# A constant two-part inverse stage on array quarters, with its twiddle factors moved into the last stage's table

## The chip, the cores and the metric

One core of one Trainium2 chip. The metric is the device time of one execution in microseconds (us). The kernel runs on one core, so there is no second die to compare; the granted TensorE clock stands beside each profile.

## The reference

The input is 8 batches of 3008 positions with 256 features. Each batch is mixed along the positions by a filter in the frequency domain, and a two-layer network with a hard swish follows. All data are float32.

```python
def _attn_ref(x, filt_r, filt_i):            # x (8, 3008, 256)
    X = np.fft.rfft(x, axis=1)
    F = (filt_r + 1j * filt_i)[None, :, :]
    y = np.fft.irfft(X * F, n=x.shape[1], axis=1)
    return y.astype(np.float32)

def _moe_ref(x, w_in, w_out):                # x (24064, 256), w_in (256, 2048)
    h = x @ w_in
    g = h * np.clip(h + 3.0, 0.0, 6.0) / 6.0
    return (g @ w_out).astype(np.float32)
```

## The kernel before

The transforms are factored, 3008 = 47 x 64. Going forward, a 47-point stage (`a_unit`, the "first stage") is followed by a 64-point stage (`b_unit`, the "second stage"). VectorE multiplies by the filter (`f_unit`, `y_unit`). Going back, `bi_unit` is the 64-point stage and `n_unit` the 47-point stage (the "last stage"), which writes straight into the network's input `xn`. Between the two inverse stages the data go through memory: `g_store` writes `g_tmp`, `t4_load` reads it back in another order.

Batch 0 is transformed ahead of everything ("the start"). Then the network runs as a loop of 376 steps (47 blocks of 512 tokens, 8 steps each), and the transforms of batches 1 to 7 are placed unit by unit into its steps. What the argument touches:

```python
psF = pool("psF", 2, space=PSUM)   # two banks, shared by a, b, bi and n units in the loop
wai = const.tile([P, TOK], FP32, name="wai")          # last stage, one table for all columns
...
def table_load(b, c):               # 4 frequencies: filter, wb and wi, three buffers each
    ...
    wi = tabp.tile([P, TC, P], FP32, name="wi")
    nc.sync.dma_start(wi, wi_d[:, ts(c, TC), :])
    st["tab", b, c] = wb, wi
...
def a_unit(b, c):                   # first stage: four 64x64 quarters of the array, two banks
    xc = x_tile(b, c)
    t = t1p.tile([P, 2, XC // 2, D], FP32, name="t1")
    ps = [bank(b) for h in range(2)]
    for g in range(2):
        for h in range(2):
            nc.tensor.matmul(ps[h][ts(g, 64)], wa[ts(h, 64), ts(g, 64)],
                             xc[ts(h, 64), 2 * g:2 * g + 2, :], start=True, stop=True)
    for h in range(2):
        nc.scalar.activation(out=t[:, h, :, :], in_=ps[h], func=AXT.Copy)
...
def bi_unit(b, i):                  # inverse second stage: 2 frequencies, own table each
    y = st.pop(("y", b, i))
    c, r = divmod(2 * i, TC)
    ps = psF.tile([P, 2, D], FP32, name="psf", tag="f")
    for u in range(2):
        nc.tensor.matmul(ps[:, u, :], st["tab", b, c][1][:, r + u, :], y[:, u, :], start=True, stop=True)
    if r == 0:
        st["t3", b, c] = t3p.tile([P, TC, D], FP32, name="t3")
    nc.scalar.activation(out=st["t3", b, c][:, r:r + 2, :], in_=ps, func=AXT.Copy)
...
# the loop's schedule of one batch (k: block in which its tokens are first used)
b_at = [(k - 2 - j // 3) * NP + 6 - 2 * (j % 3) for j in u]
bi_at = [i + 3 for i in b_at]
a_at = [(k - 7 + c // 4) * NP + (0, 2, 5, 7)[c % 4] for c in range(NB)]
if n == 1:                          # batch 1 has less room and is packed densely
    a_at = list(range(NB))
    b_at = [10 + 7 * i // 4 for i in range(NU)]
    bi_at = [i + 3 for i in b_at]
```

## Time and profile before

| | before |
|---|---|
| three runs, median (range) | 2824.01 us (2823.33 to 2826.01) |
| profiled run | 2821.93 us, span 2820.1 us, granted clock 0.982 |
| start, up to the first matmul of the loop | 133.76 us |
| loop steps 0 to 8; 8 to 34 (batch 1); 34 to 375 (batches 2 to 7) | 77.12; 195.38; 2383.19 us |
| rest | 30.68 us |

The stretches are differences between the starts of loop steps, and a step starts with the first matmul that reads `xn` into `al`. These five terms add up to the span.

From the table of groups with each shape kept apart: line, engine, operation, output<-inputs, tile, count, then busy us and mean ns of one, then the idle time ahead of them and its releasers. The first is the unit that is changed, the second the first-stage unit of the same shape as the new one, the third the eviction.

```profile
L305 PE MATMUL psf<-y,wi 128*128 128x256 f32 x384 | 106.0, 401 | 25.7 <-DVE y L297 17.9 <-issue 7.9
L252 PE MATMUL psf<-xs,wa 64*64 64x512 f32 x448 | 68.7, 623 | 0.0
L308 ACT ACTIVATE t<-psf 128x512 f32<-128x512 f32 x96 | 57.3, 597 | 102.7 <-PE psf L305 99.7 <-DMA g_tmp<-t 3.0
```

The idle 25.7 us before L305 is mostly in the start, where TensorE waits for VectorE. Busy time of quarter matmuls overlaps (448 records in 68.7 us, though one takes 623 ns), so what such a unit costs must be read from the step it sits in.

### The profile page before, as it was taken

Reading aid. Unit: us, or ns where it says so; the run is one execution under the profiler, and the core shown is the slowest. Engines: PE = TensorE matmul, PEld = TensorE weight load, DVE = VectorE, ACT = ScalarE, POOL = GpSimd, SP = SyncE. Lnnn points to the kernel's source line nnn. Section 1 sums busy time; section 2 is a strip of 40 time slices with the busy share of each in tenths; the row PEclk is TensorE's granted clock in tenths of the full one; section 3 lists DMA queues with packets and bytes.
Section 4 is the critical chain, followed back from the end, with each engine's and each line's share of the span. In section 5 each row is a group of like instructions: output and inputs, shape, how many; then the busy total and the mean of one; then the engine's idle time right before and its main releaser. Section 6 shows DMA issues by size and latency. Waiting matters only on the chain.

```text
span 2820.1 us, 47236 instructions
## 1 busy us (share of the span) xinstructions
PE 2713.0 (96%) x18096; PEld 2461.9 (87%) x18096; DVE 1991.3 (71%) x3463; ACT 1329.8 (47%) x2672; POOL 437.3 (16%) x621
## 2 busy tenths in 40 slices
PE   4589999999999999999999999999999999999997
PEld 1369898999889998899988999899998999999996
DVE  6787865777657776677756777567775677766665
ACT  1144455444554445544455444544455444444443
POOL 6470012000120011201021101210012100000000
PEclk7699999999999999999999999999999999999998
DMA  8543223311223222422134211342113421100000
GB/s 241 160 121 104 79 58 104 103 54 54 81 73 101 59 65 70 105 68 80 40 86 108 68 60 45 88 112 75 48 48 92 110 67 47 42 24 24 17 8 16
DMA packets 127817, 211.89 MB, mean 75 GB/s; under 512 B 22280, under 2 KB 86600, under 8 KB 127592
## 3 DMA queue, kind: packets, MB, share of 16 engines
q1 hardware_dynamic: 103892, 150.54, 18.9%
q0 software_dynamic: 19104, 52.46, 6.5%
q10 hardware_dynamic: 4596, 5.88, 0.6%
q8 instruction: 143, 2.34, 0.3%
q14 instruction: 82, 0.67, 0.1%
HBM read 133.81 MB, written 74.97 MB: 74 GB/s over the span
## 4 chain that ended last, share of the span: by engine, by line
PE 92%; DMA 3%; DVE 2%; POOL 1%; issue 1%; ACT 0%; SPq 0%; ACTq 0%; POOLq 0%; DVEq 0%
PE po L440 41%; PE al L364 23%; PE be L364 17%; PE psn L339 4%; PE psf L305 3%; PE psf L277 3%; PE psf L252 2%; DMA z_tmp<-t 1%; DMA xn<-in_x_dram 1%; DMA ft<-in_filt_i_dram 0%; DMA xs<-in_x_dram 0%; DVE y L296 0%; ACT t L255 0%; DVE y L297 0%; DVE s L291 0%
## 5 line engine op out<-in xcount | busy, mean ns | idle before, releaser
L440 PEld LDWEIGHTS po<-w_out,g 128*128 128x128 f32 x10528 | 1402.0, 192 | 123.0 <-DVE g L422 31.6
L440 PE MATMUL po<-w_out,g 128*128 128x128 f32 x10528 | 1426.6, 276 | 5.0 <-DVE g L414 4.6
L414 DVE SCALAR_TENSOR_TENSOR g<-r,h 128x512 f32<-128x512 f32 x752 | 518.3, 689 | 255.7 <-ACT r L409 242.8
L409 ACT ACTIVATE r<-h,half_c 128x512 f32<-128x512 f32 x752 | 542.5, 721 | 318.0 <-DVE h L390 305.7
L364 PE MATMUL al<-xt,w_in 128*128 128x256 f32 x2256 | 676.0, 382 | 6.6 <-DVE h L395 4.4
L390 DVE TENSOR_TENSOR h<-be,s 128x512 f32<-128x512 f32 x376 | 259.7, 691 | 277.8 <-PE be L364 271.6
L364 PE MATMUL be<-xn,w_in 128*128 128x256 f32 x1504 | 447.8, 379 | 0.0
L364 PEld LDWEIGHTS al<-xt,w_in 128*128 128x128 f32 x2256 | 342.9, 192 | 10.2 <-DVE h L395 4.5
L404 ACT ACTIVATE h<-al 128x256 f32<-128x256 f32 x376 | 144.0, 383 | 375.9 <-PE al L364 375.9
L364 PEld LDWEIGHTS be<-xn,w_in 128*128 128x128 f32 x1504 | 286.2, 190 | 38.9
L395 DVE TENSOR_TENSOR h<-al,s 128x256 f32<-128x256 f32 x376 | 159.4, 424 | 192.9 <-PE al L364 192.5
L422 DVE TENSOR_TENSOR g<-g 128x512 f32<-128x512 f32 x376 | 260.3, 692 | 12.9
L385 ACT ACTIVATE s<-al 128x256 f32<-128x256 f32 x376 | 144.3, 384 | 202.1 <-PE al L364 202.1
L376 ACT ACTIVATE s<-be 128x256 f32<-128x256 f32 x376 | 144.0, 383 | 182.6 <-PE be L364 182.6
L364 PE MATMUL al<-xn,w_in 128*128 128x256 f32 x752 | 225.2, 381 | 0.5 <-ACT h L404 0.5
L364 PE MATMUL be<-xt,w_in 128*128 128x256 f32 x752 | 224.3, 380 | 0.8 <-POOL xt L357 0.8
L265 POOL DMA_DIRECT2D z_tmp<-t x224 | 132.7, 595 | 426.7 <-ACT t L255 423.7
L424 DVE TENSOR_TENSOR g<-g 128x256 f32<-128x256 f32 x376 | 168.8, 449 | 12.8
L375 ACT ACTIVATE s<-al 128x256 f32<-128x256 f32 x376 | 144.0, 383 | 70.8 <-PE al L364 70.7
L421 DVE TENSOR_TENSOR g<-g 128x256 f32<-128x256 f32 x376 | 161.9, 430 | 12.8
L364 PEld LDWEIGHTS be<-xt,w_in 128*128 128x128 f32 x752 | 143.0, 190 | 20.8 <-POOL xt L357 1.6
L357 POOL TENSOR_TENSOR xt<-xn 128x256 f32<-128x256 f32 x94 | 71.4, 759 | 495.0 <-ACT xn L345 495.0
(71 smaller groups left out, 1825.3 us busy)
## 6 DMA issues: line engine op xcount, KB each, us to landing
t<-z_tmp SPq DMA_DIRECT2D x48, 512.0 KB
t<-g_tmp SPq DMA_DIRECT2D x188, 120.0 KB
z_tmp<-t POOLq DMA_DIRECT2D x224, 96.0 KB, 2.9
g_tmp<-t POOLq DMA_DIRECT2D x42, 512.0 KB, 3.4
out_dram<-o SPq DMA_DIRECT2D x328, 47.0 KB
xs<-in_x_dram SPq DMA_DIRECT2D x120, 128.0 KB
ft<-in_filt_r_dram SPq DMA_DIRECT2D x96, 128.0 KB
ft<-in_filt_i_dram SPq DMA_DIRECT2D x96, 128.0 KB
```

The source lines that it names most:

```text
L364: nc.tensor.matmul(ps, w_in[p][:, w, :], x, start=start, stop=stop, skip_group_check=True)
L375: nc.scalar.activation(out=s[:, 0, :], in_=al, func=AXT.Copy)
L376: nc.scalar.activation(out=s5, in_=be[:, 1, :], func=AXT.Copy)
L385: nc.scalar.activation(out=s[:, 1, :], in_=al, func=AXT.Copy)
L390: nc.vector.tensor_tensor(out=st["h"][0].rearrange("p (a n) -> p a n", a=2), in0=be, in1=s, op=ALU.add)
L395: nc.vector.tensor_tensor(out=st["h"][1][:, 256:512], in0=al, in1=s5, op=ALU.add)
L409: nc.scalar.activation(out=r, in_=st["h"][i], func=AXT.Relu, bias=half_c, scale=1.0 / 6.0)
L414: nc.vector.scalar_tensor_tensor(out=st["g", k, p][:, o:o + 2, :].rearrange("p a n -> p (a n)"), in0=st["r", i], scalar=1.0, in1=st["h"][i ...
L421: v.tensor_tensor(out=g[:, G1, :], in0=g[:, G3, :], in1=g[:, G22, :], op=ALU.add)
L422: v.tensor_tensor(out=g[:, G3:G2 + 1:2, :], in0=g[:, G3:G1 + 1, :], in1=g[:, G11:G11 + 1, :].broadcast_to([P, 2, 256]), op=ALU.subtract)
L424: v.tensor_tensor(out=g[:, G4, :], in0=g[:, G12, :], in1=g[:, G2, :], op=ALU.subtract)
L440: nc.tensor.matmul(st["po", k][bank][:, part, u, :], g[:, a, ts(u, P)], w_out[p][:, w, :], start=(p == 0 and n in OPENS and u == 0), stop= ...
```

## The change

The old inverse 64-point stage multiplied the two parts (real and imaginary) of each frequency by a 128x128 table of its own, because the twiddle factors were folded in. The change leaves them out of this stage. What stays is one constant table, `wi` [128, 64], of 33 cosine and 31 sine columns: its upper 64 rows multiply the real half of `y`, its lower 64 rows the imaginary half, and the two results are kept apart. So one pair of units (four frequencies) becomes four 64x64 matmuls over 512 columns, one on each quarter of the array. The two row halves write two PSUM banks, and the pair therefore takes both banks of the pool. (The Trainium skill, "TensorEngine Tiling (Array Packing)", section Gotcha 1: PSUM Pressure, says that row tiles must write different banks.) The twiddles, and the sums and differences that put columns c and 64 - c back together, go into the last stage's table `wai`, which now has 32 slices, one for each such pair of columns.

```diff
-    wai = np.zeros((P, TOK))
+    wai = np.zeros((P, HC, TOK))          # HC = 32 columns, twiddles inside
-    wi = np.zeros((P, KH, P))
+    wi = np.zeros((P, NC))                # rows of the real half over rows of the imaginary half
...
-    g_d = nc.dram_tensor("g_tmp", (B, KH, P, D), FP32, kind="Internal").ap()
+    g_d = nc.dram_tensor("g_tmp", (B, NU, 2, 2, NC, D), FP32, kind="Internal").ap()
...
     def bi_unit(b, i):
-        y = st.pop(("y", b, i))
-        ...
-        ps = psF.tile([P, 2, D], FP32, name="psf", tag="f")
-        for u in range(2):
-            nc.tensor.matmul(ps[:, u, :], st["tab", b, c][1][:, r + u, :], y[:, u, :], start=True, stop=True)
-        ...
-        nc.scalar.activation(out=st["t3", b, c][:, r:r + 2, :], in_=ps, func=AXT.Copy)
+        ys = [st.pop(("y", b, i + v)) for v in range(2)]
+        ps = [psF.tile([P, 2, D], FP32, name="psf", tag="f") for ri in range(2)]
+        for v in range(2):
+            for ri in range(2):
+                nc.tensor.matmul(ps[ri][ts(v, 64)], wi[ts(ri, 64), :], ys[v][ts(ri, 64)], start=True, stop=True)
+        t = t3p.tile([P, 2, 2, D], FP32, name="t3")
+        for ri in range(2):
+            nc.scalar.activation(out=t[:, ri, :, :], in_=ps[ri], func=AXT.Copy)
+        st["t3", b, i] = t
...
     def g_store(b, i, q=None):
-        q.dma_start(g_d[b, ts(c, TC), :, :].rearrange("k p d -> p k d"), st.pop(("t3", b, c)))
+        for v in range(2):
+            q.dma_start(g_d[b, i + v].rearrange("ri u c d -> c (ri u) d"), t[ts(v, 64)].rearrange("p ri u d -> p (ri u) d"))
...
     def t4_load(i, k0=0, k1=KH):
-                nc.sync.dma_start(t4[i % 2][p0 + k0:p0 + k1, 0:n, :], g_d[b, k0:k1, ds(ri * NC + h * HC + j, n), :])
+                nc.sync.dma_start(t4[i % 2][p0 + k0:p0 + k1, 0:n, :].rearrange("k j d -> k (j d)"),
+                                  g_d[b, k0 // 2:k1 // 2, ri, :, ds(h * HC + j, n), :].rearrange("i u j d -> i u (j d)"))
...
     def n_unit(i, dh):
-            nc.tensor.matmul(ps[:, ts(q, TOK)], t4[i % 2][:, q, ts(dh, P)], wai, start=True, stop=True)
+            nc.tensor.matmul(ps[:, ts(q, TOK)], t4[i % 2][:, q, ts(dh, P)], wai[:, chunks[i][1] + q, :], start=True, stop=True)
```

The rest (cut): filter and `wb` tables have two buffers in place of three and no `wi` load, `wai` is loaded once (1.5 MB), output rows are written through `outer(j, h)`, and in batches 2 to 7 the pair is placed alone in its step.

More of the change, by code (lines that the diff above doesn't have):

```diff
@@ L35 @@
 TB = 3
+FB = 2
+T3B = 2
 NU = KH // 2
@@ L42, with outer @@
 RING = 3 * BLK
+def outer(j, h):
+    return (NC - j if j else HC) if h else j
 def _make_tables():
@@ L55, in _make_tables @@
                 wa[h * 64:h * 64 + NA, g * 64 + 32 + k] = -np.sin(th)
-            m = 2.0 if k else 1.0
-            wai[h * 64 + k, h * NA:(h + 1) * NA] = m * np.cos(th)
-            wai[h * 64 + 32 + k, h * NA:(h + 1) * NA] = -m * np.sin(th)
     wb = np.zeros((P, KH, P))
-    wi = np.zeros((P, KH, P))
+    wi = np.zeros((P, NC))
     re, im = slice(0, NC), slice(NC, P)
@@ L70, in _make_tables @@
             wb[re, k, HALF + q], wb[im, k, HALF + q] = -sn, sign * cs
-            wi[q, k, re], wi[q, k, im] = cs, sign * sn
-            wi[HALF + q, k, re], wi[HALF + q, k, im] = -sn, sign * cs
+    for q in range(64):
+        g, sign = (q, 1.0) if q < 32 else (31 - q, -1.0)
+        co, si = (f([2 * np.pi * ((j * g) % NC) / NC for j in range(HC + 1)]) for f in (np.cos, np.sin))
+        ab = np.concatenate([co, np.zeros(HC - 1) if q == 63 else si[1:HC]])
+        wi[q], wi[HALF + q] = ab, sign * ab
+    for j in range(HC):
+        for h in range(2):
+            to = slice(h * NA, (h + 1) * NA)
+            for k in range(KH):
+                m = 2.0 if k else 1.0
+                th = 2 * np.pi * ((a * k * NC + outer(j, h) * k) % N) / N
+                cs, sn = m * np.cos(th), m * np.sin(th)
+                s = -1.0 if h else 1.0
+                if j:
+                    wai[k, j, to], wai[32 + k, j, to] = cs, -sn
+                    wai[64 + k, j, to], wai[96 + k, j, to] = -s * sn, -s * cs
+                else:
+                    wai[h * 64 + k, j, to], wai[h * 64 + 32 + k, j, to] = cs, -sn
     f = np.float32
@@ L105 @@
     t2p = pool("t2p", TB)
-    tabp = pool("tabp", TB)
+    tabp = pool("tabp", FB)
     sp = pool("sp", 2)
     yp = pool("yp", 3)
-    t3p = pool("t3p", 2)
+    t3p = pool("t3p", T3B)
     xtp = pool("xtp", 2)
@@ L120 @@
     wa = const.tile([P, P], FP32, name="wa")
-    wai = const.tile([P, TOK], FP32, name="wai")
+    wai = const.tile([P, HC, TOK], FP32, name="wai")
+    wi = const.tile([P, NC], FP32, name="wi")
     xs = [const.tile([P, XC, D], FP32, name="xs%d" % i) for i in range(3)]
-    ft = [const.tile([P, TC, D], FP32, name="ft%d" % i) for i in range(TB)]
+    ft = [const.tile([P, TC, D], FP32, name="ft%d" % i) for i in range(FB)]
     t4 = [const.tile([P, NJ, D], FP32, name="t4%d" % i) for i in range(2)]
@@ L137, in table_load @@
     def table_load(b, c):
-        t = ft[(b * NT + c) % TB]
+        t = ft[(b * NT + c) % FB]
         for src, p0 in ((filt_r, 0), (filt_i, HALF)):
@@ L144, in table_load @@
         nc.sync.dma_start(wb, wb_d[:, ts(c, TC), :])
-        wi = tabp.tile([P, TC, P], FP32, name="wi")
-        nc.sync.dma_start(wi, wi_d[:, ts(c, TC), :])
-        st["tab", b, c] = wb, wi
+        st["wb", b, c] = wb
     NCONV = 16
@@ L276, in b_unit @@
         for u in range(2):
-            nc.tensor.matmul(ps[:, u, :], st["tab", b, c][0][:, r + u, :],
+            nc.tensor.matmul(ps[:, u, :], st["wb", b, c][:, r + u, :],
                              st["t2", b, c][:, r + u, :], start=True, stop=True)
@@ L283, in f_unit @@
         ps = st.pop(("ps", b, i))
-        f = ft[(b * NT + c) % TB][:, r:r + 2, :]
+        f = ft[(b * NT + c) % FB][:, r:r + 2, :]
         s1 = sp.tile([P, 2, D], FP32, name="s1")
@@ L300, in bi_unit, with g_store @@
     def bi_unit(b, i):
-        y = st.pop(("y", b, i))
-        c, r = divmod(2 * i, TC)
-        ps = psF.tile([P, 2, D], FP32, name="psf", tag="f")
-        for u in range(2):
-            nc.tensor.matmul(ps[:, u, :], st["tab", b, c][1][:, r + u, :], y[:, u, :], start=True, stop=True)
-        if r == 0:
-            st["t3", b, c] = t3p.tile([P, TC, D], FP32, name="t3")
-        nc.scalar.activation(out=st["t3", b, c][:, r:r + 2, :], in_=ps, func=AXT.Copy)
-    def g_store(b, c, q=None):
+        ys = [st.pop(("y", b, i + v)) for v in range(2)]
[7 more added lines that the diff above has]
+        st["t3", b, i] = t
+    def g_store(b, i, q=None):
         q = q or nc.gpsimd
-        q.dma_start(g_d[b, ts(c, TC), :, :].rearrange("k p d -> p k d"), st.pop(("t3", b, c)))
+        t = st.pop(("t3", b, i))
+        for v in range(2):
+            q.dma_start(g_d[b, i + v].rearrange("ri u c d -> c (ri u) d"), t[ts(v, 64)].rearrange("p ri u d -> p (ri u) d"))
     chunks = []
@@ L479, in out_5 @@
             m = min(NA - a, P - p)
-            nc.sync.dma_start(raw(out, b * N + a * NC + h * HC + j, [[NC * D, m], [1, D]]),
+            nc.sync.dma_start(raw(out, b * N + a * NC + outer(j, h), [[NC * D, m], [1, D]]),
                               o[p:p + m, t % BLK // P, :])
@@ L527 @@
         convert(6)
+        nc.sync.dma_start(wi, wi_d)
         for c in range(TB):
             t2_load(0, c)
-            if c:
+            if 0 < c < FB:
                 table_load(0, c)
-        nc.sync.dma_start(wai, wai_d)
         for t in t4:
@@ L542 @@
             if i:
-                bi_unit(0, i - 1)
                 if i % 2 == 0:
+                    bi_unit(0, i - 2)
                     c = i // 2 - 1
-                    g_store(0, c, nc.scalar)
+                    g_store(0, i - 2, nc.scalar)
+                    if c + FB < NT:
+                        table_load(0, c + FB)
+                    if c == 0:
+                        nc.sync.dma_start(wai, wai_d)
                     if c + TB < NT:
                         t2_load(0, c + TB)
-                        table_load(0, c + TB)
                     if c == NT - 2:
@@ L585, in places @@
             b_at = [(k - 2 - j // 3) * NP + 6 - 2 * (j % 3) for j in u]
-            bi_at = [i + 3 for i in b_at]
+            bi_at = [b_at[i] + (5 if i % 6 == 1 else 3) for i in range(NU)]
             a_at = [(k - 7 + c // 4) * NP + (0, 2, 5, 7)[c % 4] for c in range(NB)]
@@ L602 @@
                 elif n > 1:
-                    at(max(prev[0][c + NB - 3], s - 6), x_load, n, c)
+                    at(max(prev[c + NB - 3], s - 6), x_load, n, c)
             for c in range(NT):
-                s = bi_at[2 * (c - TB) + 1] if c >= TB else a_at[-1] + 1
-                if n > 1 and c < TB:
-                    s = max(s, prev[1][2 * (NT + c - TB) + 1])
+                s = b_at[2 * (c - TB) + 1] + 1 if c >= TB else a_at[-1] + 1
+                at(s, t2_load, n, c)
+                s = b_at[2 * (c - FB) + 1] + 1 if c >= FB else a_at[-1] + 1
                 at(s, table_load, n, c)
-                at(s, t2_load, n, c)
             for i in range(NU):
@@ L613 @@
                 at(b_at[i] + 1, y_unit, n, i)
-                at(bi_at[i], bi_unit, n, i)
                 if i % 2:
-                    at(bi_at[i], g_store, n, i // 2)
-            prev = a_at, bi_at
+                    at(bi_at[i], bi_unit, n, i - 1)
+                    at(bi_at[i], g_store, n, i - 1)
+            prev = a_at
         items = [(k, p) for k in range(NBLK) for p in range(NP)]
```

## The prediction

> **What bounds the kernel now.** I read the granted clock first: one core, 0.982, so no throttled state to correct for. Then the busy totals, the slices and the chain of work that ended last.
>
> ```profile
> PE 2713.0 (96%) x18096; PEld 2461.9 (87%) x18096; DVE 1991.3 (71%) x3463; ACT 1329.8 (47%) x2672; POOL 437.3 (16%) x621
> ...
> PE   4589999999999999999999999999999999999997
> ...
> PEclk7699999999999999999999999999999999999998
> ...
> PE 92%; DMA 3%; DVE 2%; POOL 1%; issue 1%; ACT 0%; SPq 0%; ACTq 0%; POOLq 0%; DVEq 0%
> ```
>
> TensorE is full from the fourth slice (about 210 us) to the last; only the first three slices are set by something else. The table of stretches says it sharper: TensorE is busy 25.44 of 30 us in 180 to 210, 30.00 of 30 in 210 to 240, and 500.00 of 500 in each of the three stretches from 1000 to 2500. So after 210 us a TensorE nanosecond removed is a nanosecond won, unless a new wait takes its place; before 210 us it isn't.
>
> What the concerned step costs I read from the order of time of TensorE. The main loop has 376 steps, each starting with the first matmul of L364 that reads xn into al. Four such starts, with what stands between:
>
> ```profile
> 1002.04 0.60 PE L364 MATMUL al<-xn,w_in 128*128 128x256 f32 x2
> ...
> 1009.05 0.60 PE L364 MATMUL al<-xn,w_in 128*128 128x256 f32 x2
> ...
> 1010.35 1.03 PE L305 MATMUL psf<-y,wi 128*128 128x256 f32 x4
> 1011.22 0.61 PE L440 MATMUL po<-w_out,g 128*128 128x128 f32 x4
> ...
> 1016.07 0.60 PE L364 MATMUL al<-xn,w_in 128*128 128x256 f32 x2
> ...
> 1022.21 0.60 PE L364 MATMUL al<-xn,w_in 128*128 128x256 f32 x2
> ```
>
> A step with one inverse unit (L305, two matmuls, four records) lasts 7.02 us, a step with nothing extra 6.14. Over all steps after the 30th the medians are 6.148 plain (86 steps), 7.012 with an inverse unit (71), 7.265 with a last-stage unit L339 of five columns, 7.365 with a first-stage unit L252 (41). Within a class they agree to some 0.001 us (one plain step is 0.06 longer): the loop has no slack and no noise. So one inverse unit costs 0.864 us, one first-stage unit 1.217.
>
> The first-stage unit matters because the new inverse unit has exactly its shape: four 64x64 by 512 matmuls, one on each quarter of the array, the two row halves into two PSUM banks.
>
> ```profile
> 840.63 0.59 PE L364 MATMUL be<-xn,w_in 128*128 128x256 f32 x2
> 841.15 1.09 PE L252 MATMUL psf<-xs,wa 64*64 64x512 f32 x8
> 842.17 0.71 PE L440 MATMUL po<-w_out,g 128*128 128x128 f32 x4
> 842.72 0.60 PE L364 MATMUL al<-xt,w_in 128*128 128x256 f32 x2
> ```
>
> From be to L252 pass 0.52 us where the usual step is 0.43, and from L440 to al 0.55 where it is 0.44: entering and leaving quarter mode costs some 0.2 us, the eight records 1.02.
>
> **What the skill says.** The Trainium skill, "TensorEngine Tiling (Array Packing)", section Key Properties, says that changing the tiling mode drains the array and that tiles operate independently: the two 0.1 us gaps and the 1.02 us for eight records agree. The same page, section PSUM Bottleneck, says that tiling speeds TensorE but not the emptying of PSUM: the 128x512 ACT evictions stay as many as they are (96 of 0.597 us on L308), and no run yet shows whether they delay. The Trainium skill, "FP8 and Floating Point Precision", section TensorE Precision Notes, gives true FP32 four passes through the array; with 262 cycles for 256 columns at 2.4 GHz ("TensorE: Matmul & The Clock Gate", section Back-to-back issue gap) two passes make 218 ns, and this trace has 0.864/4 = 216 ns per record, two records per matmul. It agrees.
>
> **The change part by part.** *Removed*: 84 inverse units after the first batch (7 batches of 12), each 0.864 us. *Added*: 42 pair units, each four quarter matmuls. Multiplications halve; by passes the four quarters need 2 records x 427 ns = 0.853 us if all run at once, against 1.728 for two old units. I take not that but the measured twin: 1.217 us. A pair saves 1.728 - 1.217 = 0.511 us. *Moved*: the twiddles go into the last stage's moving operand, which gets a different slice per column but the same shape 128x94, so L339 stays at 1.117 us for five. VectorE work is unchanged; evictions are as many and as large. Stores to g become 84 of 64 partitions in place of 42 of 128, the bytes the same, from GpSimd, which is 16% busy. Table loads lose wi (48 loads of 256 KB) and their buffers go from three to two; in the loop a table is asked for seven or more steps (over 40 us) ahead, so that costs nothing. wai grows from 47 KB to 1.5 MB, loaded once in the first stage, where six wi loads of the same total disappear.
>
> *Batches 2 to 7*: the schedule puts all 36 pairs alone in their step. 36 x 0.511 = 18.4 us saved.
>
> *Batch 1* is packed more densely. Counting which units share a step, five of its six pairs meet another user of the two-buffer PSUM pool in the same step (two behind a last-stage unit, two ahead of a second-stage unit, one ahead of a first-stage unit). A pair takes both buffers, so someone waits for an ACT eviction. The trace prices that: last-stage plus first-stage in one step lasts 9.229 where the sum is 6.148 + 1.117 + 1.217 = 8.482, a wait of 0.747. Removed 12 x 0.864 = 10.4, added 6 x 1.217 = 7.3 plus 5 x 0.75 = 3.8: a loss of about 0.7. That stretch also shows VectorE waits (steps 24 to 26), so I book a loss of 0.5.
>
> *Start, before 210 us.* From 60 to 118 us VectorE is nearly gapless (filter products and weight conversion), so TensorE's gain there is nothing. Its end is a serial chain:
>
> ```profile
> 117.86 0.70 DVE y L297
> ...
> 118.69 1.12 PE psf L305 x4
> ...
> 119.83 0.60 ACT t L308
> ...
> 120.46 3.74 DMA g_tmp<-t
> ...
> 124.55 2.77 DMA t<-g_tmp
> ```
>
> The pair now ends with two evictions after the last y instead of one (+0.6), two stores issued 0.4 us apart instead of one, and, from the order of the changed program, ten instead of eight small loads behind that store (2 x 0.34 us). GpSimd's conversion runs beside it and hides some. I book a loss of 1.5 us. The filter tables with two buffers: the third chunk's can be issued when VectorE leaves the first (66 us), is needed at 79.6, and a load takes 5 to 7 us here; no wait.
>
> Sum: 2824.0 - 18.4 + 0.5 + 1.5 = 2807.6 us, 0.6% less.
>
> **The rivals.**
> 1. *The PSUM pool eats the gain everywhere.* Twelve of the 36 pairs follow directly on a step with a second-stage unit, whose buffer VectorE frees only with its third product:
>
> ```profile
> 1051.95 0.69 DVE L291 TENSOR_TENSOR s<-psf,ft 64x512 f32<-64x512 f32 x1
> ...
> 1052.93 1.03 PE L305 MATMUL psf<-y,wi 128*128 128x256 f32 x4
> ```
>
> The buffer is free at 1052.64, 0.29 us before the pair would start; VectorE to TensorE hand-over is about 0.15 (79.60 to 79.75 in the start). It fits, narrowly. Were it missed by 0.3 us each time, 4 us go: 2811. Two evictions in a row on ACT (1.2 us) before the next step's s could also hold L390; against it, first-stage units evict twice too and their steps show the plain sum. If every pair waited the 0.75, the change would lose 36 x 0.24 = 9 us: 2833 or so.
> 2. *The start gets slower.* Two filter buffers, and loads that wait on the completion of a store eight transfers back, as the fourth chunk's load does now (its second quarter waits 6.4 us until 73.5). If the larger wai transfer or the later paired stores delay each of the last three tables by 3 us, 2816. For it: that stretch moves 250 GB/s at 0.86 DMA share. Against: every need I could date has 5 us or more of slack.
> 3. *Better than the twin.* If the quarters came at their pass count plus a mode change (0.85 + 0.2), a pair saves 0.66, and 36 give 24: 2802. The twin's own count speaks against it.
>
> **Range and chances.** The body is a product of two durations that do not scatter, so most of the spread is the start (about 4 us either way) and rival 1. Range 2800 to 2816. For 2% the kernel would have to lose or gain 56 us, three times all that the changed unit can save; even the removal of every inverse matmul would save but 84 x 0.864 = 73. Faster by over 2%: 0.01; within: 0.97; slower: 0.02.
>
> **What would show each step.** A step with a pair alone at 7.36 us (7.0 to 7.3 would favour rival 3, 8.1 rival 1); the new inverse rows at about 42 x 1.2 us beyond the start; pairs directly behind a second-stage unit no longer than the others; waits of first bank writes on ACT evictions only in steps 14, 18, 25, 28 and 32; the main loop's first matmul at 135 us rather than 133.8 (140 or more would be rival 2); the three 500 us stretches holding the same 100% TensorE. The prediction is wrong if the pair's step isn't 7.36, or if the first 210 us move by more than 4.

## More of the kernel before

The loads that read `g_tmp` back, all issued by SyncE, with the issue times of one in ns (min/median/max):

```profile
L333 SPq DMA_DIRECT2D t<-g_tmp x236: 239/362/1230, 117.9 to 2622.2; - x118
```

## The result, and the profile after

| | before | after |
|---|---|---|
| median of 4 runs (range) | 2823.67 us (2823.21 to 2826.01) | 2807.19 us (2805.65 to 2807.47) |
| ratio to before, 95% interval | | 0.9939 [0.9922, 0.9956]: within 2% |
| profiled run, granted clock | 2821.93 us, 0.982 | 2807.47 us, 0.987 |
| start | 133.76 | 138.21 |
| steps 0 to 8 | 77.12 | 75.35 |
| steps 8 to 34 (batch 1) | 195.38 | 196.50 |
| steps 34 to 375 | 2383.19 | 2364.89 |
| rest | 30.68 | 30.74 |

The kernel is 0.6% faster, and the gain has one place: steps 34 to 375, 18.30 us. The start up to step 8 gave back 213.56 - 210.88 = 2.68 us and batch 1 1.12 us.

The page of the changed kernel: TensorE is as full as before, with 13 us less work, and the chain of work that ended last is TensorE by the same 92%.

```profile
PE 2700.1 (96%) x18096; PEld 2395.8 (85%) x18096; DVE 1993.9 (71%) x3463; ACT 1325.9 (47%) x2672; POOL 456.4 (16%) x663
...
PE   3589999999999999999999999999999999999997
...
PEclk9699999999999999999999999999999999999998
...
PE 92%; DVE 3%; DMA 2%; ACT 1%; issue 1%; POOL 0%; SPq 0%; ACTq 0%; POOLq 0%; DVEq 0%
```

The count of TensorE records is the same, 18096, because two records per 256-column matmul became two per 512-column quarter matmul; only their kind changed. Memory reads fell from 133.81 to 122.75 MB, which the table loads account for, and no time follows from that, as the experiments show.

The order of time of TensorE in the changed kernel, around a step that holds a pair and nothing else (start us, duration us, engine, line, operation, output<-inputs, tile, count):

```profile
1013.55 0.60 PE L392 MATMUL al<-xn,w_in 128*128 128x256 f32 x2
...
1019.70 0.60 PE L392 MATMUL al<-xn,w_in 128*128 128x256 f32 x2
...
1020.56 0.59 PE L392 MATMUL be<-xn,w_in 128*128 128x256 f32 x2
1021.09 1.09 PE L329 MATMUL psf<-y,wi 64*64 64x512 f32 x8
1022.11 0.71 PE L468 MATMUL po<-w_out,g 128*128 128x128 f32 x4
1022.66 0.60 PE L392 MATMUL al<-xt,w_in 128*128 128x256 f32 x2
...
1027.06 0.60 PE L392 MATMUL al<-xn,w_in 128*128 128x256 f32 x2
```

The plain step lasts 6.15 us, the step with the pair 7.36. The 0.53 us from `be` to L329 and 0.55 from L468 to `al` are, within 0.01 us, those that the prediction read around the first-stage unit. Over all 36 steps with a pair alone the duration is 7.364 to 7.365 us, also for those right behind a step with a second-stage unit. No step of the loop beyond batch 1 waits for anything new.

The groups of the changed kernel, in the order of those shown of before:

```profile
L329 PE MATMUL psf<-y,wi 64*64 64x512 f32 x384 | 73.0, 648 | 13.9 <-DVE y L319 13.7 <-DVE s L314 0.3
L275 PE MATMUL psf<-xs,wa 64*64 64x512 f32 x448 | 68.4, 623 | 0.7 <-ACT t L332 0.7
L332 ACT ACTIVATE t<-psf 128x512 f32<-128x512 f32 x96 | 52.8, 596 | 95.6 <-PE psf L329 83.8 <-DMA ft<-in_filt_r_dram 11.3
```

The unit's busy time fell from 106.0 to 73.0 us, and its twin L275 stays as it was. The 0.7 us before L275 waiting for L332 is one shared step of batch 1.

What batch 1 pays is seen in its step 25, which starts at 339.55 and lasts 10.32 us, where the sum of its parts is 6.148 + 1.217 + 0.864 = 8.23. The order of time of TensorE in the changed kernel, with the idle time and its releaser in brackets:

```profile
339.55 0.60 PE L392 MATMUL al<-xn,w_in 128*128 128x256 f32 x2
...
340.94 1.07 PE L329 MATMUL psf<-y,wi 64*64 64x512 f32 x2
342.27 1.08 PE L329 MATMUL psf<-y,wi 64*64 64x512 f32 x6 [0.27 <-DVE s L314]
344.05 1.13 PE L300 MATMUL psf<-t,wb 128*128 128x256 f32 x4 [0.69 <-ACT t L332]
```

The pair gets its first bank and then waits for VectorE to free the second, which a second-stage unit still holds. The next second-stage unit (L300) waits 0.69 us for the pair's eviction. The five steps with such a meeting, 14, 18, 25, 28 and 32, exceed the sum of their parts by 0.75, 1.09, 2.09, 0.69 and 1.05 us. Of this, 0.67 us in step 25 and 0.75 in step 32 were there before the change. Steps 17, 19 and 26 exceed theirs by 0.60, 0.69 and 1.66 us in both kernels.

In the start, the chain of work that ended last, in order of time, from the last pair on (start us, us, what):

```profile
119.20 2.70 PE psf L329 x4
...
121.93 0.60 ACT t L332
...
122.55 3.29 DMA g_tmp<-t
...
125.86 0.73 SPq L360
...
126.64 0.73 SPq L360
...
127.41 0.65 SPq L360
...
128.11 0.61 SPq L360
...
128.77 0.59 SPq L360
...
129.40 2.94 DMA t<-g_tmp
```

Against the chain of before that the prediction shows, two pieces grew. The matmuls ahead of the eviction take 2.70 us in place of 1.12. Part of that is waiting: the chain of before starts at the end of the last `y` product, this one at the end of the last but one, because the matmuls on the real half can start then. Those on the imaginary half wait for the last product (L320), as the order of time of TensorE's weight loads shows:

```profile
119.92 0.28 PEld L329 LDWEIGHTS psf<-y,wi 64*64 64x64 f32 x2 [0.44 <-DVE y L320]
```

From the end of the last `y` to that of the matmuls it is 2.02 us against 1.25 before, 0.77 more; the table of stretches has a granted clock of 0.50 in 118 to 122 us here and 0.75 before. And between the store's landing and the last load's issue SyncE is on the chain with five issues of 0.59 to 0.73 us: 3.5 us from 125.86 to 129.36, where the chain of before has one issue of 0.24. Every load of this line has become slower to issue, in the loop too:

```profile
L360 SPq DMA_DIRECT2D t<-g_tmp x236: 589/748/967, 119.4 to 2609.0; - x118
```

So 2.68 us of loss have a suspect that the prediction did not have: the pattern of these loads.

### The profile page after: what moved, and what is told of

It is laid out like the page before. It is cut to its first block, busy times and chain, and to the rows that moved or that the text cites. A ratio compares the mean times of both kernels' runs of the same rounds, so it can differ in the third digit from the quotient of the medians.

```text
span 2805.7 us, 47214 instructions
## 1 busy us (share of the span) xinstructions
PE 2700.1 (96%) x18096; PEld 2395.8 (85%) x18096; DVE 1993.9 (71%) x3463; ACT 1325.9 (47%) x2672; POOL 456.4 (16%) x663
## 3 DMA queue, kind: packets, MB, share of 16 engines
HBM read 122.75 MB, written 74.97 MB: 70 GB/s over the span
## 4 chain that ended last, share of the span: by engine, by line
PE 92%; DVE 3%; DMA 2%; ACT 1%; issue 1%; POOL 0%; SPq 0%; ACTq 0%; POOLq 0%; DVEq 0%
PE po L468 41%; PE al L392 23%; PE be L392 17%; PE psn L367 4%; PE psf L300 3%; PE psf L275 2%; PE psf L329 2%; DMA z_tmp<-t 1%; DVE g L442 0%; DVE y L319 0%; DMA g_tmp<-t 0%; DMA xn<-in_x_dram 0%; DVE s L314 0%; DVE s L313 0%; ACT t L278 0%
## 5 line engine op out<-in xcount | busy, mean ns | idle before, releaser
L468 PEld LDWEIGHTS po<-w_out,g 128*128 128x128 f32 x10528 | 1398.3, 192 | 152.4 <-issue 37.3
L468 PE MATMUL po<-w_out,g 128*128 128x128 f32 x10528 | 1430.6, 276 | 4.9 <-DVE g L442 4.6
L495 POOL TENSOR_TENSOR o<-p,o 128x256 f32<-128x256 f32 x47 | 34.1, 725 | 878.1 <-ACT t L332 361.3
```

Source lines behind the costliest of these rows:

```text
L468: nc.tensor.matmul(st["po", k][bank][:, part, u, :], g[:, a, ts(u, P)], w_out[p][:, w, :], start=(p == 0 and n in OPENS and u == 0), stop= ...
```

## The experiments

The theory: the gain is the step count times 0.511 us, because a pair runs four quarters at once (half the passes) and pays a mode change; what is lost in batch 1 is the two banks that a pair takes; what is lost in the start is the loads' pattern. Rivals: the gain comes from the table loads that are gone; the quarters do not overlap fully and the mode change is small; the start is lost to the two stores, or to two filter buffers. The runs e1 to e4 were made on one chip (before there: 2823.35 us, 7 runs), e0, e5, e6 and e7 on a second (before: 2823.39, 7 runs), e8 on a third (before: 2822.91, 9 runs). All results were correct.

### The change without quarters (e1_full)

The constant table is put block-diagonal into a full 128x128 array. Table loads, twiddles in the last stage and two filter buffers stay as in the change; the layout of `g_tmp`, its loads and its single store are those of before.

```diff
-    wi = np.zeros((P, NC))
+    wi = np.zeros((P, P))
-        wi[q], wi[HALF + q] = ab, sign * ab
+        wi[q, :NC], wi[HALF + q, NC:] = ab, sign * ab
         for v in range(2):
-            for ri in range(2):
-                nc.tensor.matmul(ps[ri][ts(v, 64)], wi[ts(ri, 64), :], ys[v][ts(ri, 64)], start=True, stop=True)
+            nc.tensor.matmul(ps[v], wi, ys[v], start=True, stop=True)
```

> The change with its mathematics, schedule and twiddle placement, but the constant cosine and sine matrices as one block-diagonal 128x128 weight on the whole array: two matmuls of 512 columns per pair instead of four on quarters; the intermediate keeps the old layout. Theory (the gain is quarter concurrency on a full TensorE): four records of 512 columns at 427 ns make 1.71 us per pair where the quarters took 1.217, so a step with a pair alone lasts 7.86 us, 36 of them cost 18 us more, and the time goes back to about 2822 (the simpler loads may give 3 us at the start). Rival (the gain is the removed table loads, or the moved twiddles): 2804 to 2808, whatever the step lasts.

Measured: 2822.18 us (2821.16 to 2823.28), ratio to before 0.9996 [0.9979, 1.0012]. The order of time of TensorE in this kernel:

```profile
1023.12 0.59 PE L389 MATMUL be<-xn,w_in 128*128 128x256 f32 x2
1023.55 1.88 PE L328 MATMUL psf<-y,wi 128*128 128x512 f32 x4
1025.27 0.61 PE L465 MATMUL po<-w_out,g 128*128 128x128 f32 x4
```

The pair's step lasts 7.865 us, 1.717 above a plain one: almost exactly two old units (1.728). Steps 34 to 375 take 2382.76 us, against 2383.19 before. So the gain of these steps is the quarters alone; the layout, which also differs here, is ruled out by e4_loads below, which has the old layout with quarters and keeps the gain. That 11 MB less are read and that the twiddles moved is worth nothing by itself; it is what makes a table with empty quarters possible.

### The quarters twice (e2_twice)

From batch 1 on, each pair runs its four matmuls twice, with the same result.

```diff
-        for v in range(2):
+        for v in [0, 1] * (2 if b else 1):
```

> Each pair of batches 1 to 7 issues its four quarter matmuls twice, the second time over the same result (the output stays right). The added cost is that of four quarter matmuls without a mode change. If all four quarters run at once, the step grows from 7.365 by 0.85 us (two records of 427 ns) and the rest of the 1.217, some 0.36, is the price of entering and leaving the mode; total about 2843. If only two quarters run at once, the step grows by 1.7. If there is no price for the mode and the quarters are just slower, it grows by 1.2.

Measured: 2846.4 us (one run). The order of time of TensorE in this kernel:

```profile
1036.17 0.60 PE L392 MATMUL be<-xn,w_in 128*128 128x256 f32 x2
1036.69 1.95 PE L329 MATMUL psf<-y,wi 64*64 64x512 f32 x16
1038.57 0.71 PE L468 MATMUL po<-w_out,g 128*128 128x128 f32 x4
```

The step lasts 8.224 us. The second four quarters cost 8.224 - 7.365 = 0.859 us, and two of the four records of e1_full, which together took 1.717 us, would be 0.859 too (the 427 ns of the expectation was an estimate): all four quarters run at once. The first four cost 1.217, so a group of quarters has a fixed price of 0.36 us, which the full-array pair of e1_full does not have (1.717 us, no more than two old units). That this price is that of going into quarter mode and back is the reading that fits; it was not separated from anything else that happens once per group. Of the 0.87 us that halving the passes would save on a pair, the fixed price takes 0.36, and 0.51 is left. The total is 3.4 us above the expected 2843, and the loop starts 3.0 us later than in the change.

### The order of the two loops (e3_order)

Both quarters of the first bank run first, then both of the second.

```diff
-        for v in range(2):
-            for ri in range(2):
+        for ri in range(2):
+            for v in range(2):
```

> The four quarter matmuls of a pair in the other order: both column halves of one row half first, then the other row half. If any two quarters run at once, the step with a pair stays 7.365 us. If only quarters of different row halves overlap, neighbours in this order block each other and the step grows by up to 0.4 us.

Measured: 2810.0 us (one run). A pair alone takes 7.365 us, as before, so the order does not touch the overlap. Where banks are short it does, as the order of time of TensorE in this kernel's step 25 shows:

```profile
342.90 1.08 PE L329 MATMUL psf<-y,wi 64*64 64x512 f32 x4
344.24 1.08 PE L329 MATMUL psf<-y,wi 64*64 64x512 f32 x4 [0.26 <-DVE s L314]
345.24 1.13 PE L300 MATMUL psf<-t,wb 128*128 128x256 f32 x4
```

Four records instead of two can run while the second bank is still held, the first bank is evicted sooner, and L300 no longer waits. Step 25 lasts 9.55 instead of 10.32 us, step 18 8.98 instead of 9.32, and batch 1 195.35 instead of 196.50. That supports the bank theory. The whole is not faster, because its start was long (140.78 us to step 0; e2_twice, whose start has no edit, had 141.21, so that is scatter) and one last-stage step was 1.37 us longer, once.

### The old pattern of the loads (e4_loads)

The eviction writes its tile in another order, so that `g_tmp` can keep its old layout and the loads their old pattern.

```diff
-    g_d = nc.dram_tensor("g_tmp", (B, NU, 2, 2, NC, D), ...)
+    g_d = nc.dram_tensor("g_tmp", (B, KH, P, D), ...)
-            nc.scalar.activation(out=t[:, ri, :, :], in_=ps[ri], func=AXT.Copy)
+            nc.scalar.activation(out=t[:, :, ri, :], in_=ps[ri], func=AXT.Copy)
-            q.dma_start(g_d[b, i + v].rearrange("ri u c d -> c (ri u) d"), ...)
+            q.dma_start(g_d[b, ts(i + v, 2)].rearrange("u (ri c) d -> c (u ri) d", ri=2), ...)
-    (t4_load: the pattern of the change)
+    (t4_load: the pattern of before)
```

> The intermediate g laid out by frequency, real or imaginary, c, so that a load of the last stage has the simple pattern it had before the change; the eviction writes its tile in the matching order. Theory for the lost start (each of these loads takes SyncE 0.59 to 0.88 us to issue in the changed kernel, 0.24 to 0.33 before, and some ten stand behind the last store): the main loop's first matmul comes about 3 us earlier, near 135 us, and the time is about 2804. Rival (the start is late for other reasons, the cold clock and the paired evictions): issue times fall but the first matmul moves by under 1 us. The steps of the loop stay as they are.

Measured: 2804.79 us (2804.32 to 2806.07), ratio to before 0.9936 [0.9921, 0.9951]. The issue times of the loads, and the end of the chain in the start, in order of time:

```profile
L360 SPq DMA_DIRECT2D t<-g_tmp x236: 240/362/783, 118.7 to 2604.7; - x118
```

```profile
122.45 3.40 DMA g_tmp<-t
...
125.87 0.24 SPq L360
...
126.15 0.29 SPq L360
...
126.49 0.29 SPq L360
...
126.83 2.65 DMA t<-g_tmp
```

The median issue is back at 362 ns, and from the store's landing to the last load's issue pass 0.9 us instead of 3.5. The loop starts at 135.35 us. Over all profiles, those with the loads' old pattern start the loop at 134.8 to 136.2 us (e1, e4, e6, e7, e8), those with the new one at 138.2 to 141.2 (the change twice, e2, e3, e5). Two stores and the slow pair (2.70 us, as in the change) are still there.

Part of that difference is scatter from before the chain: the last `y` product ends anywhere from 118.5 to 123.2 us. From its end to step 0 pass 15.22 us before and 15.34 in e1; 16.00 to 16.28 with quarters, two stores and the old loads (e4, e6, e7, e8); and 18.34 to 20.04 with the new loads (the change twice, e3, e5; in e2, with 18.00, the chain runs through GpSimd instead). So the pattern of the loads is the larger part of the start's loss, 2 to 4 us, and pair and stores together are about 1. The total time alone would not show it: 2804.3 to 2806.1 us here and 2805.7 to 2807.5 for the change overlap. Steps 34 to 375 are 2364.89 us, the same to the hundredth.

### The changed kernel once more (e0_after)

No edit; it gives the other three runs of its chip something to stand beside.

> The changed kernel again, as the base of this call: 2805.5 to 2807.5 us; the main loop's first matmul somewhere between 138 and 141 us, since two runs with the same first batch as this kernel began at 141 and its own profile at 138.

Measured: 2808.35 us (2808.21 to 2808.89), ratio to before 0.9949 [0.9934, 0.9964], a little above the expected range. Batch 1 (196.50) and steps 34 to 375 (2364.89) repeat to 0.01 us; the start was 139.50 instead of 138.21. Between these two executions the whole scatter is in the start.

### Another schedule for batch 1 (e5_batch1)

Each pair of batch 1 gets a step without another user of the two banks.

```diff
-                b_at = [10 + 7 * i // 4 for i in range(NU)]
-                bi_at = [i + 3 for i in b_at]
+                b_at = [10, 11, 14, 15, 17, 19, 20, 23, 25, 27, 28, 30]
+                bi_at = [13, 13, 18, 18, 22, 22, 26, 26, 29, 29, 33, 33]
```

> Only the schedule of batch 1 changed: second-stage units at steps 10, 11, 14, 15, 17, 19, 20, 23, 25, 27, 28, 30 and pairs at 13, 18, 22, 26, 29, 33, so that no pair shares its step with another user of the two-buffer PSUM pool. Theory (the waits in steps 14, 18, 25, 28 and 32 are for that pool, 5.7 us over the sum of their parts): steps 8 to 33 shrink by 5 to 8 us, the time is 2799 to 2802. Rival (the waits are VectorE's, which has the same products to do in the same stretch): the waits move to other steps and under 2 us are won.

Measured: 2804.67 us (2803.75 to 2810.04), ratio to before 0.9939 [0.9925, 0.9954]. Batch 1 takes 193.75 instead of 196.50 us: 2.75 won, about half of what was expected. The waits for evictions are gone, but waits for VectorE took part of their place, as the order of time of TensorE in this kernel shows for its step 25:

```profile
341.26 1.03 PE L300 MATMUL psf<-t,wb 128*128 128x256 f32 x4
...
345.22 1.16 PE L468 MATMUL po<-w_out,g 128*128 128x128 f32 x8 [0.30 <-DVE o L494]
```

TensorE waits there for VectorE, which has filter products on its queue beside the loop's own work. Steps 16, 17 and 21 wait for the loop's own VectorE work in the same way. In steps 18, 26 and 29, longer by 0.33, 0.33 and 1.21 us, the pair stands directly behind a second-stage unit and still waits for a bank: VectorE frees it late (L314). Seven steps of the stretch (16, 17, 18, 21, 25, 26 and 29) are longer than their parts, by 5.9 us in all. In the changed kernel the five meetings (5.7 us) and the three steps of both kernels (2.9 us) came to 8.6: the schedule removed the five meetings, and about 3 us came back in steps that wait for VectorE. So VectorE is what batch 1 waits for next.

### Both repairs (e6_both)

The edits of e4_loads and e5_batch1 together.

> The simple last-stage loads and the new schedule of batch 1 together: if they are independent, the sum of the two gains, about 2.4 + 6, so 2797 to 2800.

Measured: 2803.09 us (2801.1 to 2805.04), ratio to before 0.9931 [0.9914, 0.9947]. The parts add up in the trace (step 0 at 136.24, batch 1 193.75, steps 34 to 375 2364.88), but the time misses the expected 2797 to 2800, because e5's gain, on which that figure rested, was half of what I had booked.

### First-stage units moved within their block (e7_first)

On top of e6: steps in which a last-stage and a first-stage unit meet last 9.23 us, 0.75 more than their parts. The edit moves the first-stage units away from them.

```diff
-            a_at = [(k - 7 + c // 4) * NP + (0, 2, 5, 7)[c % 4] for c in range(NB)]
+            a_at = [(k - 7 + c // 4) * NP + (0, 1, 2, 5)[c % 4] for c in range(NB)]
```

> As the one before, and the first-stage units of batches 2 to 7 at steps 0, 1, 2, 5 of their blocks instead of 0, 2, 5, 7, where six of them meet a last-stage unit and wait 0.747 us for its eviction. If that wait is only for the PSUM pool, 6 x 0.747 = 4.5 us more go: about 2794. If the earlier units wait for their loads or stores instead, nothing is won.

Measured: 2805.91 us (2803.81 to 2806.75), ratio to before 0.9939 [0.9924, 0.9954]: no gain over e6, which took 2803.09, where about 2794 was expected. Steps 39, 87, 135 and so on fell from 9.23 to 7.26 us, but steps 33, 81, 129 and so on rose from 7.37 to 9.63. The order of time of TensorE in this kernel at such a step:

```profile
400.47 1.09 PE L329 MATMUL psf<-y,wi 64*64 64x512 f32 x8
402.26 1.57 PE L275 MATMUL psf<-xs,wa 64*64 64x512 f32 x8 [0.70 <-ACT t L332]
```

I had moved a first-stage unit onto a step that holds the last pair of the batch before. Two units that each take both banks meet there, and the second waits 0.70 us for an eviction. It is the same cost, met in another place, and a mistake in my reading of the schedule.

### First-stage units spread over free steps (e8_spread)

On top of e6, with the first-stage units only on steps that hold neither a last-stage unit nor a pair.

```diff
-            a_at = [(k - 7 + c // 4) * NP + (0, 2, 5, 7)[c % 4] for c in range(NB)]
+            a_at = [(k - 7) * NP + o for o in (0, 2, 5, 8, 9, 10, 13, 15)]
```

> The simple loads, the new schedule of batch 1, and the first-stage units of batches 2 to 7 at steps 0, 2, 5, 8, 9, 10, 13, 15 of their two blocks, where none meets a last-stage unit or a pair (the run before this one put one of them on the previous batch's last pair by mistake). If the 0.747 us in six steps is only the wait for the PSUM pool, 4.5 us go against the version with loads and batch 1 alone: about 2798.5. If first-stage units in three consecutive steps wait for their loads or stores, less or nothing.

Measured: 2798.43 us (2795.64 to 2800.1), ratio to before 0.9912 [0.9898, 0.9926]. Steps 34 to 375 fell from 2364.88 to 2360.22 us, by 4.66; six steps (one in each of batches 2 to 7) of 0.747 make 4.48 of it. This is the fastest version by its median, 0.9% below before; against the change it ran on another chip, and all of these differences are within 2%. This last edit has nothing to do with the change, and the kernel before has the same 9.23 us steps; I did not run it there.

## Why the prediction was right

The predicted time, 2807.6 us, and the measured one, 2807.19, agree more closely than the working deserves. By its own terms, on the two profiles:

| term of the sum | predicted | measured |
|---|---|---|
| batches 2 to 7 | -18.4 | -18.30 |
| batch 1 | +0.5 | +1.12 |
| start (to step 8) | +1.5 | +2.68 |
| rest | 0 | +0.06 |
| sum | -16.4 | -14.44 |

The medians differ by 16.5 us and these profiles by 14.4, because single executions of a kernel differ by some microseconds, and where two profiles could be compared the difference lay in the start (138.21, 139.50 and 141.21 us to step 0 in three profiles with the same start). That the landing is 0.4 us off is partly that luck.

**What bounds the kernel** was read rightly for the body: TensorE, with no slack. It holds from step 34 (about 410 us) and not quite from the 210 us that the busy shares suggested: in batch 1 some steps wait for VectorE in both kernels (17, 19 and 26, by 2.9 us). From step 34 on the durations of the steps that the pairs are in are the sum of their units, before and after, and 18.30 of the 18.4 us arrived.

**The price of the pair** was taken from the first-stage unit of the same shape and not from the pass count. It was right to the nanosecond (7.365 us), and e2 shows why the pass count alone would have been wrong: full overlap, 0.859 us, plus the fixed 0.36. The prediction's reading of some 0.2 us for the mode change, which is this fixed price, from two gaps between the recorded starts, was too small; the rest of it hides in the records' own 1.02 us, which is more than the 0.859 that eight records need when the mode does not change. Rival 3 had used that reading, and it fell for this reason.

**Rival 1**, the PSUM pool, did not happen in batches 2 to 7: pairs right behind a second-stage unit were no longer than others. It happened in batch 1, in exactly the five steps named. The term there was too small, because five equal waits of 0.75 were booked and the sum rounded down. Measured, the five meetings cost 5.66 us, of which 1.42 had been there before, so 4.24 is new: 7.3 + 4.24 - 10.4 makes 1.14, and the stretch shows 1.12. The waits were not alike. A pair ahead of a second-stage unit can wait on both sides (step 25), and the last meeting replaced one that cost 0.75 already.

**The start** is where a cost was missing. The prediction counted ten loads where eight had been, at the old 0.34 us of issue, and none of the changed patterns. Each took 0.59 us or more; e4 showed that the pattern is the cause. The prediction's own sign for the start, the loop's first matmul at 135 us, failed: it came at 138.21, and in e2 and e3 past the 140 that was to mean rival 2. Of the 4.45 us that step 0 is late, 1.32 were there at the last `y` product already, which scatters between executions, and 3.12 came after it. The second eviction, booked with 0.6 us, cost nothing, because the first ran while the second bank was still being filled, but the matmuls behind the last `y` took 0.77 us more, at a granted clock of 0.50. In e2, whose start is the same program and whose clock was 0.94 in 122 to 125 us, they took 1.12 us in place of 2.02, so the low clock is enough to explain it; why it is low in one execution and not in another is not shown. From step 0 to step 8 the changed kernel recovered 1.77 us of its 4.45: 0.85 us of it is a wait of the kernel before for a GpSimd result in step 0, which in the changed kernel is ready when TensorE comes; the rest I did not follow up. Rival 2 was half right about the place and wrong about its cause; the two filter buffers made SyncE wait longer (23.1 us for VectorE in the first 140 us, against 2.7 before), and VectorE never waited for a table in the start.

## What to carry to other kernels

Price a new operation by one of the same shape that is already in the trace, at its cost per step and not at its pass count; here the twin was right to the nanosecond. Quarters of the array halve the passes but pay a fixed price for a group, so put as many quarter matmuls together as the banks allow; and a unit that takes both buffers of a two-buffer pool must be alone in its step, or one meeting gives back all that a pair saves (0.7 us or more against 0.51). When a layout in memory changes, look at every transfer that reads it: an extra dimension in a load's pattern can double its issue time, which counts wherever loads stand on a serial chain.

## What the Trainium skill lacked or had wrong

- "TensorEngine Tiling (Array Packing)", section Key Properties, says that a change of tiling mode drains the array but gives no price. Here a group of four float32 64x64x512 matmuls has a fixed cost of 0.36 us, read as entering and leaving the mode (1.217 us for the first four, 0.859 for four more in the same mode). Its other sentence, that tiles work independently, agrees: four quarters at once in the time of one.
- The same page, section PSUM Bottleneck, warns of the eviction in general. Here it cost nothing in 36 steps with a pair alone, and 0.7 to 2.1 us in each of five steps where another unit shared the two banks; moving the units apart removed the waits for evictions with as many evictions as before (e5), so the two banks are the limit and not the eviction's throughput. No run gave the pool a third bank.
- "DMA: Bandwidth & Descriptors", section Latency and other measured facts, has a first-byte latency for transfers issued from SyncE, but no page that I found has this chip's issue time by access pattern. For the same 120 KB loads it was 362 ns in the median with the plain pattern and 748 ns with one dimension more.
